# Grouped-query attention on one Trainium2 core: VectorE turns the keys of units 4, 7, 10 and every third up to 28, q1 starts in unit 3, query weights come by halves of the heads, and o is scaled in one instruction

## The chip, the cores and the metric

The kernel runs on one core of a Trainium2 chip. The metric is the device time of one execution in microseconds. Six runs of the kernel before took 185.41 to 186.72 us, with a median of 185.89 us. Engines are named as in the profile: PE (TensorE, with PEld for its weight loads), DVE (VectorE), ACT (ScalarE), POOL (GpSimd) and SP (SyncE, which issues nearly all loads).

## The reference

```python
B, Sq, D = 8, 32, 1024
Hq, Hkv, Sk, Dh = 32, 4, 8192, 128
W = 2048                                   # min(4096, max(256, Sk // 4))
q = (x @ wq) split into 32 heads of 128
k, v = the last W positions of k_cache, v_cache; each of the 4 kv heads serves 8 query heads
scores = q @ k^T * Dh ** -0.5
o = softmax(scores) @ v
out = o (heads side by side, 4096 wide) @ wo
```

All inputs and the output are bf16.

## The kernel before, in words

The work is 32 units: one unit is one batch row b and one kv head g, with the eight batch rows of g = 0 first. A unit has 256 query columns (8 heads x 32 positions) and 2048 keys, which are 16 blocks of 128. It runs in four *slots* (the loop over `c` in `run`, lines 462 to 488), so there are 128 slots. In a slot PE makes the transposed scores of four key blocks (L467, `s_ps`: K turned is the stationary side, q the moving side), ACT takes exp into `pT` (L469), and PE multiplies `pT` of two slots earlier with `va` (L478, `o_ps`). `va` is V with a column of ones beside it, so `o_ps` also holds the sum of the exponentials. `va_copy` (L409) copies V there on DVE at the start of each unit, into one of three buffers. When a unit's last product is issued, `finish_unit` (lines 411 to 424) runs on DVE: a reciprocal of the sums (L415), two scalings of 128x128 into `o_sb` (L420), and a transpose in blocks of 32 into `OT` (L422).

The other work of PE is cut into pieces that are put in slots behind the slot's own matmuls:

- `q_pieces` (lines 267 to 280) make q of the next kv head g: per head two pieces of four 128x256 matmuls (L275) and one DVE copy into `QT` (L278). `Q_SLOTS` (L30) spreads the 16 pieces of g = 1 over slots 17 to 31. A head of g needs both halves of that head group's weights, which are halves of the contraction (`load_wq`, L156), rows of 2 KB.
- `o_pieces` (L282) multiply finished heads with `wo` (L295) and add into `oacc`.
- `k_pieces` (lines 224 to 239) turn the keys of the units in `PE_T` on PE, four 128x128 transposes in each slot of the unit before (L236), and DVE copies half a unit at a time from PSUM to `kT` (L238).

Keys come in transposed in one of three ways. Units in `PE_T` are turned by PE from a plain load (`k_raw`). Units in `V_T` are turned by DVE and POOL from a plain load (`kv_pieces`, lines 241 to 262): four DVE transposes in blocks of 32 (L251), then sixteen moves of 32x512 that put the blocks in their places. A move reads a part of all four transposed pieces, so none can start before the fourth. In `V_T` stand, for each unit, the unit whose load brings `k_raw` along, the slots of the four transposes, the first and last slot of the moves, and how many of the moves POOL does (L261); DVE does the rest (L259). All other units use the DMA's transposing load, in two halves (L196).

Every engine's order is that in which the program is written: a slot's side pieces decide where an instruction stands in its engine's queue. SP issues the loads in the order of `load_unit` (line 207), about five units ahead; `W_AT` (L28) says with which unit each of 28 pieces of weights is issued. An SP instruction waits for a free buffer and for the transfer eight before it.

Buffers that matter: 2 for `k_raw` of units 0 and 1 and for `kTv` (the result of `kv_pieces`), 4 for other `k_raw`, 5 for `kT`, 6 for V, 6 for weights, 2 PSUM banks each for scores, `o_ps` pairs and side work.

Of the kernel before, what the change touches and what calls it, by code (L numbers as in the profile page):

```python
# [9 lines left out]
ALU = mybir.AluOpType  # L10
AX = mybir.AxisListType
BF16 = mybir.dt.bfloat16
FP32 = mybir.dt.float32
# [7 lines left out]
VA_ROW = 160  # L21
V_HALVES = 30

PE_T = (0, 1, 2, 3, 4)

V_T = {5: (2, (5, 6, 8, 10), 10, 17, 12),
       **{u: (u - 4, range(4 * u - 16, 4 * u - 12), 4 * u - 13, 4 * u - 4, 16) for u in (8, 11, 14, 17, 20, 23, 26, 29)}}
W_AT = (3, 3, 4, 4, 8, 8, 9, 9, 11, 12, 13, 13, 14, 15, 16, 16, 18, 19, 19, 20, 22, 22, 23, 24, 25, 26, 28, 28)  # L28

Q_SLOTS = {1: (17, 31), 2: (38, 54), 3: (69, 83)}  # L30
O_SLOTS = {0: (54, 71), 1: (84, 101), 2: (99, 123), 3: (124, 143)}


# [71 lines left out]
class Fast:  # L105
# [50 lines left out]
    def load_wq(self, g, half, cuts=(2, 2)):  # L156
# [8 lines left out]
                                   in_=self.wq[:, g * GW:(g + 1) * GW].rearrange("(p c) n -> p c n", p=P)[:, c0:c0 + n, :])  # L165
        return [lambda i=sum(cuts[:k]), n=n: piece(i, n) for k, n in enumerate(cuts)]

    def load_wo(self, gq):

        def piece(i):  # L170
            if i == 0:
                self.wo_t[gq] = self.wp.tile([self.P, 4, self.D], BF16, name="wo_sb", tag="w")
            r0 = gq * 4 * self.Dh
            self.nc.sync.dma_start(out=self.wo_t[gq][:, 2 * i:2 * i + 2, :],
                                   in_=self.wo[r0:r0 + 4 * self.Dh, :].rearrange("(p c) n -> p c n", c=4)[:, 2 * i:2 * i + 2, :])
        return [lambda i=i: piece(i) for i in range(2)]
# [30 lines left out]
    def load_unit(self, ui):  # L207

        if ui < len(self.units):
            if ui not in V_T:  # L210
                self.load_k(ui, None if ui in PE_T else 0)
            self.load_v(ui, self.nc.sync)
            if ui not in V_T and ui not in PE_T:
                self.load_k(ui, 1)
        for u, at in V_T.items():
            if at[0] == ui:
                self.load_k(u)
        for p, at in zip(self.weights, W_AT):
            if at == ui:
                p()  # L220

    def k_pieces(self, ui):

        if ui not in PE_T:
            return []
# [13 lines left out]
    def kv_pieces(self, ui):  # L241


        nc, P, KT = self.nc, self.P, self.KT
        st = {}

        def blocks(i):
            if i == 0:
                st["kb"] = self.kbp.tile([P, KT, P], BF16, name="kb")
            sl = slice(i * KT // 4, (i + 1) * KT // 4)  # L250
            nc.vector.transpose(out=st["kb"][:, sl, :], in_=self.k_raw[ui][:, sl, :])  # L251

        def move(k, d):
            if k == d == 0:
                self.kT[ui] = self.kvt.tile([P, KT, P], BF16, name="kTv", tag="kv")
            out = self.kT[ui][d * 32:(d + 1) * 32, :, k * 32:(k + 1) * 32]
            in_ = st["kb"][k * 32:(k + 1) * 32, :, d * 32:(d + 1) * 32]
            if d >= V_T[ui][4] // 4:
                nc.vector.tensor_copy(out=out, in_=in_)  # L259
            else:  # L260
                nc.gpsimd.tensor_scalar(out=out, in0=in_, scalar1=1.0, scalar2=1.0, op0=ALU.mult, op1=ALU.mult)  # L261
        return [lambda i=i: blocks(i) for i in range(4)], [lambda k=k, d=d: move(k, d) for k in range(4) for d in range(4)]
# [4 lines left out]
    def q_pieces(self, g):  # L267
        nc, P, DC = self.nc, self.P, self.DC
        st = {}

        def piece(hl, i):
            if i == 0:
                st["ps"] = self.ps_m.tile([P, 512], FP32, name="q_ps", tag="m")
            for c in range(i * DC // 2, (i + 1) * DC // 2):
                nc.tensor.matmul(st["ps"][:, 0:self.NQ], lhsT=self.wq_t[g, i][:, c % (DC // 2), hl * P:(hl + 1) * P],  # L275
                                 rhs=self.xT[:, c, :], start=(c == 0), stop=(c == DC - 1))
            if i == 1:
                nc.vector.tensor_copy(out=self.q_view(g)[:, :, hl, :],  # L278
                                      in_=st["ps"][:, 0:self.NQ].rearrange("p (b s) -> p b s", b=self.B))
        return [lambda h=h, i=i: piece(h, i) for h in range(self.rep) for i in range(2)]  # L280

    def o_pieces(self, g, t, cuts=(512, 512), st=None):  # L282
# [29 lines left out]
    def start(self):  # L312
        nc, P = self.nc, self.P
# [18 lines left out]
        self.weights = []  # L332
        for g in range(self.Hkv):
            if g + 1 < self.Hkv:
                self.weights += self.load_wq(g + 1, 0) + self.load_wq(g + 1, 1)
            if g:
                self.weights += self.load_wo(2 * g - 2) + self.load_wo(2 * g - 1)
        self.weights += self.load_wo(2 * self.Hkv - 2) + self.load_wo(2 * self.Hkv - 1)
        for ui in range(2, 4):
            self.load_unit(ui)  # L340
        for v in self.va:
            nc.gpsimd.memset(v[:, :, self.Dh:self.VW], 1.0)
        nc.gpsimd.memset(self.ones_c[:, :], 1.0)
# [67 lines left out]
    def finish_unit(self, ui, o_ps):  # L411
        nc, P, Dh, QT_N = self.nc, self.P, self.Dh, self.QT_N
        b, g = self.units[ui]
        rl = self.RL_all
        nc.vector.reciprocal(out=rl[:, ui * QT_N:(ui + 1) * QT_N], in_=o_ps[:, :, Dh])  # L415
        if ui == len(self.units) - 1:
            self.check_units(ui, ui + 1)
        o_sb = self.ob.tile([P, QT_N, 4, 32], BF16, name="o_sb")
        for qt in range(QT_N):
            nc.vector.tensor_scalar(out=o_sb[:, qt, :, :], in0=o_ps[:, qt, 0:Dh].rearrange("p (i c) -> p c i", c=4),  # L420
                                    scalar1=rl[:, ui * QT_N + qt:ui * QT_N + qt + 1], scalar2=None, op0=ALU.mult)
        nc.vector.transpose(out=self.OT[:, g * QT_N:(g + 1) * QT_N, :, b * self.Sq:(b + 1) * self.Sq], in_=o_sb[:, :, :, :])  # L422
        if ui == len(self.units) - 2:
            self.check_units(0, ui + 1)
# [20 lines left out]
    def run(self):  # L445
        nc, P, NCH, CJ, UQ, QT_N, KT = self.nc, self.P, self.NCH, self.CJ, self.UQ, self.QT_N, self.KT
        self.start()
        plan = self.side_plan()
        for i, p in enumerate(self.q_rest):
            plan[i // 2].append(p)  # L450
        pv_queue = []

        loads = {8: [4, 5, 6, 7], **{4 * (u - 5): [u] for u in range(8, len(self.units))}}

        for ui, (b, g) in enumerate(self.units):
            nxt = self.k_pieces(ui + 1)
            va = self.va[ui % 3]
            if ui:
                self.va_copy(ui)
            q_u = self.QT[g][:, b * UQ:(b + 1) * UQ]  # L460
            acc = {}
            for c in range(NCH):
                for u in loads.get(ui * NCH + c, []):
                    self.load_unit(u)
                s_ps = self.ps_s.tile([P, CJ, UQ], FP32, name="s_ps")
                for jj in range(CJ):
                    nc.tensor.matmul(s_ps[:, jj, :], lhsT=self.kT[ui][:, c * CJ + jj, :], rhs=q_u, start=True, stop=True)  # L467
                pT = self.ptp.tile([P, CJ, UQ], BF16, name="pT")
                nc.scalar.activation(out=pT[:, :, :], in_=s_ps[:, :, :], func=ACT.Exp, bias=0.0, scale=self.scale)  # L469

                def pv(c=c, pT=pT, acc=acc, va=va, ui=ui):
                    if c == 0:
                        acc["o"] = self.ps_o.tile([P, QT_N, 256], FP32, name="o_ps")
                    o_ps = acc["o"]
                    for jj in range(CJ):
                        j = c * CJ + jj
                        for qt in range(QT_N):
                            nc.tensor.matmul(o_ps[:, qt, 0:self.VW], lhsT=pT[:, jj, qt * P:(qt + 1) * P], rhs=va[:, j, 0:self.VW],  # L478
                                             start=(j == 0 and qt == 0), stop=(j == KT - 1), skip_group_check=True)
                    if c == NCH - 1:  # L480
                        self.finish_unit(ui, o_ps)
                pv_queue.append(pv)
                while len(pv_queue) > 2:
                    pv_queue.pop(0)()
                for k in ((c,) if ui else ((), (), (0, 1), (2, 3))[c]) if nxt else ():
                    nxt[k]()
                for p in plan[ui * NCH + c]:
                    p()
        after = [p for s in range(len(self.units) * NCH, len(plan)) for p in plan[s]]
        pv_queue.pop(0)()  # L490
        for p in after[:2]:
            p()
        self.pv_last, self.after = pv_queue.pop(0), after[2:]
# [162 lines left out]
```

## Time and profile before

| | |
|---|---|
| median of 6 runs | 185.89 us (185.41 to 186.72) |
| the profiled execution | 185.5 us |
| its span (first to last instruction) | 183.7 us |
| granted TensorE clock | 0.999 |
| L467 scores, PE | 368 + 144 matmuls of 128x256 |
| L478 products with V, PE | 1024 matmuls of 128x129 |
| L236 transposes of keys, PE | 64 of 128x128 |
| L469 exp, ACT | 128 x 1025 ns |
| L261 moves, POOL | 140, 669 ns mean |
| L420 scaling, DVE | 64 x 346 ns |
| L278 q copies, DVE | 24 x 407 ns |

A row of a timeline has the start and the length in microseconds, the engine, the line, the operation, what is written and read, how often, and in brackets the idle time before it with what ended it. A group row has the busy time, the mean of one in ns, and after the second bar the idle time. Matmuls overlap, so their lengths add to more than the time; the distance between two starts is what one costs. Slot 12 below is the thirteenth group of score matmuls from the start; slots 16 and 20 begin units 4 and 5.

### The profile page before, as it was taken

To read this page: it belongs to the slowest core of one execution; us is meant where nothing else is said; L and a number is where in the kernel's file an instruction comes from. 1 tells how busy PE (TensorE), PEld (TensorE's weight loads), DVE (VectorE), ACT (ScalarE), POOL (GpSimd) and SP (SyncE) were. 2 spreads that over 40 slices of the span, in tenths; PEclk is the share of its full clock that TensorE was granted. 3 is DMA by queue.
4 is the path that set the end of the run, shared out by engine and by line. 5 is a ranking of instruction groups with operands and counts; after the bars stand their busy time and mean duration, and the time that the engine had idled before them with its cause. 6 is when DMAs were issued, how large, how long until landed. Compare 5 with 4: busy or idle time off the path is not lost.

```text
span 183.7 us, 5041 instructions
## 1 busy us (share of the span) xinstructions
PE 179.4 (98%) x2041; PEld 154.0 (84%) x2057; DVE 115.8 (63%) x266; ACT 131.6 (72%) x133; POOL 94.6 (51%) x150
## 2 busy tenths in 40 slices
PE   8999999999999999999999999999999999999994
PEld 2999999999999999987878999988787888888843
DVE  0238899986685685685467558647755865365363
ACT  2208898777889787878787677787877888888800
POOL 2000009759839959929944980796299279600000
PEclk9999999999999999999999999999999999999999
DMA  5999999999999999999999999999999999990003
GB/s 193 331 411 407 400 401 379 199 210 385 268 338 253 345 298 206 393 266 318 302 380 252 338 375 236 283 261 414 231 326 400 251 270 337 241 234 9 0 30 91
DMA packets 52953, 51.72 MB, mean 282 GB/s; under 512 B 39744, under 2 KB 40256, under 8 KB 52928
## 3 DMA queue, kind: packets, MB, share of 16 engines
q1 hardware_dynamic: 52352, 50.90, 99.6%
q10 hardware_dynamic: 576, 0.49, 0.8%
q8 instruction: 15, 0.25, 0.5%
q14 instruction: 10, 0.08, 0.2%
HBM read 41.42 MB, written 0.52 MB: 228 GB/s over the span
## 4 chain that ended last, share of the span: by engine, by line
PE 98%; issue 0%; DVE 0%
PE o_ps L478 32%; PE s_ps L467 31%; PE op_ps L295 14%; PE q_ps L275 11%; PE q_ps L375 4%; PE tp L236 2%; PE warm_ps L346 2%; PE xT_ps L354 1%; PE kf_ps L368 1%; DVE o_t L305 0%; PE cnt_ps L532 0%
## 5 line engine op out<-in xcount | busy, mean ns | idle before, releaser
L469 ACT ACTIVATE pT<-s_ps 128x1024 bf16<-128x1024 f32 x128 | 128.7, 1025 | 32.7 <-PE s_ps L467 31.8
L261 POOL TENSOR_SCALAR kTv<-kb 32x512 bf16<-32x512 bf16 x140 | 93.7, 669 | 64.4 <-PE s_ps L467 37.6
L478 PE MATMUL o_ps<-va,pT 128*128 128x129 bf16 x1024 | 78.8, 220 | 0.1
L478 PEld LDWEIGHTS <-pT 128*128 128x128 bf16 x1024 | 68.5, 98 | 3.1
L467 PE MATMUL s_ps<-QT,kT 128*128 128x256 bf16 x368 | 55.2, 273 | 0.2
L467 PEld LDWEIGHTS <-kT 128*128 128x128 bf16 x368 | 34.8, 98 | 10.3
L295 PE MATMUL op_ps<-wo_sb,OT 128*128 128x512 bf16 (+2 forms) x128 | 32.7, 353 | 0.6
L275 PE MATMUL q_ps<-xT,wq_sb 128*128 128x256 bf16 x192 | 28.2, 273 | 0.0
L409 DVE COPY va<-v_sb 128x2048 bf16<-128x2048 bf16 x32 | 26.1, 817 | 0.1
L251 DVE STREAM_TRANSPOSE kb<-k_raw 128x512 bf16<-128x512 bf16 x36 | 23.8, 685 | 0.5 <-DMA k_raw<-in_k_cache_dram 0.4
L415 DVE RECIPROCAL RL_all<-o_ps 128x2 f32<-128x2 f32 x32 | 5.3, 164 | 27.0 <-PE o_ps L478 27.0
L467 PE MATMUL s_ps<-QT,kTv 128*128 128x256 bf16 x144 | 21.6, 273 | 0.0
L420 DVE TENSOR_SCALAR o_sb<-o_ps,RL_all 128x128 bf16<-128x128 f32 x64 | 19.5, 346 | 1.1
L467 PEld LDWEIGHTS <-kTv 128*128 128x128 bf16 x144 | 13.9, 98 | 5.1
L275 PEld LDWEIGHTS <-wq_sb 128*128 128x128 bf16 x192 | 17.0, 98 | 1.2
L278 DVE CAST QT<-q_ps 128x256 bf16<-128x256 f32 x24 | 9.8, 407 | 12.7 <-PE q_ps L275 12.7
L422 DVE STREAM_TRANSPOSE OT<-o_sb 128x256 bf16<-128x256 bf16 x32 | 14.2, 445 | 1.1
L295 PEld LDWEIGHTS <-OT 128*128 128x128 bf16 x144 | 11.4, 98 | 2.3 <-DVE OT L422 0.2
L302 DVE TENSOR_TENSOR oacc<-op_ps,oacc 128x512 f32<-128x512 f32 x8 | 5.5, 682 | 7.4 <-PE op_ps L295 7.4
L375 PE MATMUL q_ps<-xT,wq_sb 128*128 128x256 bf16 (+1 forms) x80 | 7.8, 251 | 0.0
L375 PEld LDWEIGHTS <-wq_sb 128*128 128x128 bf16 x80 | 6.6, 98 | 0.7 <-DMA wq_sb<-in_wq_dram 0.2
L236 PE MATMUL tp<-ident,k_raw 128*128 128x128 bf16 x64 | 5.9, 219 | 0.0
(30 smaller groups left out, 37.6 us busy)
## 6 DMA issues: line engine op xcount, KB each, us to landing
v_sb<-in_v_cache_dram SPq DMA_DIRECT2D x30, 512.0 KB, 7.2
wo_sb<-in_wo_dram SPq DMA_DIRECT2D x16, 512.0 KB, 6.9
wq_sb<-in_wq_dram SPq DMA_DIRECT2D x13, 512.0 KB, 7.2
k_raw<-in_k_cache_dram SPq DMA_DIRECT2D x13, 512.0 KB, 6.4
wq_sb<-in_wq_dram SPq DMA_DIRECT2D x6, 256.0 KB, 4.9
v_sb<-in_v_cache_dram SPq DMA_DIRECT2D x4, 256.0 KB, 4.2
kT<-in_k_cache_dram SPq DMA_TRANSPOSE x36, 7.1
k_raw<-in_k_cache_dram SPq DMA_DIRECT2D x2, 256.0 KB, 6.7
```

What stands on the lines that cost most here:

```text
L251: nc.vector.transpose(out=st["kb"][:, sl, :], in_=self.k_raw[ui][:, sl, :])
L261: nc.gpsimd.tensor_scalar(out=out, in0=in_, scalar1=1.0, scalar2=1.0, op0=ALU.mult, op1=ALU.mult)
L275: nc.tensor.matmul(st["ps"][:, 0:self.NQ], lhsT=self.wq_t[g, i][:, c % (DC // 2), hl * P:(hl + 1) * P], rhs=self.xT[:, c, :], start=(c == ...
L278: nc.vector.tensor_copy(out=self.q_view(g)[:, :, hl, :], in_=st["ps"][:, 0:self.NQ].rearrange("p (b s) -> p b s", b=self.B))
L295: nc.tensor.matmul(ps[:, 0:w], lhsT=self.OT[:, gq, c, t * P:(t + 1) * P], rhs=self.wo_t[gq][:, c, n0:n0 + w], start=(k == 0), stop=(k == 7))
L375: nc.tensor.matmul(qs[h // 2][:, h % 2, n0:n1], lhsT=self.wq_t[0, c // H][:, c % H, h * P:(h + 1) * P], rhs=self.xT[:, c, n0:n1], start=(c ...
L409: self.nc.vector.tensor_copy(out=self.va[ui % 3][:, :, 0:self.Dh], in_=self.v_sb[ui][:, :, :])
L420: nc.vector.tensor_scalar(out=o_sb[:, qt, :, :], in0=o_ps[:, qt, 0:Dh].rearrange("p (i c) -> p c i", c=4), scalar1=rl[:, ui * QT_N + qt:ui ...
L422: nc.vector.transpose(out=self.OT[:, g * QT_N:(g + 1) * QT_N, :, b * self.Sq:(b + 1) * self.Sq], in_=o_sb[:, :, :, :])
L467: nc.tensor.matmul(s_ps[:, jj, :], lhsT=self.kT[ui][:, c * CJ + jj, :], rhs=q_u, start=True, stop=True)
L469: nc.scalar.activation(out=pT[:, :, :], in_=s_ps[:, :, :], func=ACT.Exp, bias=0.0, scale=self.scale)
L478: nc.tensor.matmul(o_ps[:, qt, 0:self.VW], lhsT=pT[:, jj, qt * P:(qt + 1) * P], rhs=va[:, j, 0:self.VW], start=(j == 0 and qt == 0), stop= ...
```

## The change: which engine turns which keys, and what moves with it

`PE_T` loses unit 4: it is now turned by DVE and POOL, with six of its sixteen moves on DVE. The other units of `V_T` are 7, 10, ... 28 instead of 8, 11, ... 29, with four of the sixteen moves on DVE instead of none, spread evenly among POOL's. Unit 5 had twelve moves on POOL; it now comes by a transposing load, and so do 8, 11, ... 29. So 19 units come by transposing loads (18 before) and four units are turned on PE (five before).

The pieces of q1 start in slot 14. Query weights of g = 1 to 3 are loaded by halves of the heads, in rows of 1 KB, and q of two heads is copied at once, by ACT. The second half of q1's weights is issued with unit 5 instead of unit 4, and weights now go ahead of `k_raw` of the same load. `k_raw` of unit 4 is loaded directly behind that of unit 2. From unit 12 on `va_copy` stands one slot earlier. The two scalings of a unit become one `tensor_tensor` with the reciprocals broadcast.

```diff
-PE_T = (0, 1, 2, 3, 4)
-V_T = {5: (2, (5, 6, 8, 10), 10, 17, 12),
-       **{u: (u - 4, range(4 * u - 16, 4 * u - 12), 4 * u - 13, 4 * u - 4, 16) for u in (8, 11, 14, 17, 20, 23, 26, 29)}}
-W_AT = (3, 3, 4, 4, 8, 8, 9, 9, 11, ...
-Q_SLOTS = {1: (17, 31), 2: (38, 54), 3: (69, 83)}
+PE_T = (0, 1, 2, 3)
+V_T = {4: (None, (6, 6, 7, 8), 8, 15, 10),
+       7: (4, (15, 16, 17, 18), 18, 26, 12),
+       **{u: (u - 4, range(4 * u - 15, 4 * u - 11), 4 * u - 12, 4 * u - 3, 12) for u in range(10, 31, 3)}}
+W_AT = (3, 3, 5, 5, 8, 8, 9, 9, 11, ...
+V_EARLY = 12
+Q_SLOTS = {1: (14, 31), 2: (38, 54), 3: (69, 83)}
...
+    def load_wq_heads(self, g, half):
+        P, DC, GW = self.P, self.DC, self.rep * self.Dh
+        n0 = g * GW + half * GW // 2
+        def piece(i):
+            if i == 0:
+                self.wq_t[g, half] = self.wp.tile([P, DC, GW // 2], BF16, name="wq_sb", tag="w")
+            cs = slice(i * DC // 2, (i + 1) * DC // 2)
+            self.nc.sync.dma_start(out=self.wq_t[g, half][:, cs, :],
+                                   in_=self.wq[:, n0:n0 + GW // 2].rearrange("(p c) n -> p c n", p=P)[:, cs, :])
+        return [lambda i=i: piece(i) for i in range(2)]
...
-            if d >= V_T[ui][4] // 4:
+            i, n = 4 * k + d, 16 - V_T[ui][4]
+            if i * n // 16 != (i + 1) * n // 16:
                 nc.vector.tensor_copy(out=out, in_=in_)
...
-            if i == 0:
-                st["ps"] = self.ps_m.tile([P, 512], FP32, name="q_ps", tag="m")
+            k, R = hl // 2, self.rep // 2
+            if i == 0 and hl % 2 == 0:
+                st["ps"] = self.ps_m.tile([P, 2, self.NQ], FP32, name="q_ps", tag="m")
...
-            if i == 1:
-                nc.vector.tensor_copy(out=self.q_view(g)[:, :, hl, :],
-                                      in_=st["ps"][:, 0:self.NQ].rearrange("p (b s) -> p b s", b=self.B))
+            if i == 1 and hl % 2 == 1:
+                nc.scalar.copy(out=self.q_view(g)[:, :, 2 * k:2 * k + 2, :].rearrange("p b h s -> p h b s"),
+                               in_=st["ps"][:, :, :].rearrange("p h (b s) -> p h b s", b=self.B))
...
-        for ui in range(2, 4):
-            self.load_unit(ui)
+        self.load_k(2)
+        self.load_k(4)
+        self.load_v(2, nc.sync)
+        self.load_unit(3)
...
-        for qt in range(QT_N):
-            nc.vector.tensor_scalar(out=o_sb[:, qt, :, :], in0=o_ps[:, qt, 0:Dh].rearrange("p (i c) -> p c i", c=4),
-                                    scalar1=rl[:, ui * QT_N + qt:ui * QT_N + qt + 1], scalar2=None, op0=ALU.mult)
+        nc.vector.tensor_tensor(out=o_sb[:, :, :, :], in0=o_ps[:, :, 0:Dh].rearrange("p q (i c) -> p q c i", c=4),
+                                in1=rl[:, ui * QT_N:(ui + 1) * QT_N].unsqueeze(2).unsqueeze(3).to_broadcast([P, QT_N, 4, 32]), op=ALU.mult)
...
-            if ui:
+            if 0 < ui < V_EARLY:
                 self.va_copy(ui)
...
+                if c == NCH - 1 and V_EARLY <= ui + 1 < len(self.units):
+                    self.va_copy(ui + 1)
```

More of the change, by code (lines that the diff above doesn't have):

```diff
@@ L22 @@
 V_HALVES = 30
-PE_T = (0, 1, 2, 3, 4)
-V_T = {5: (2, (5, 6, 8, 10), 10, 17, 12),
-       **{u: (u - 4, range(4 * u - 16, 4 * u - 12), 4 * u - 13, 4 * u - 4, 16) for u in (8, 11, 14, 17, 20, 23, 26, 29)}}
-W_AT = (3, 3, 4, 4, 8, 8, 9, 9, 11, 12, 13, 13, 14, 15, 16, 16, 18, 19, 19, 20, 22, 22, 23, 24, 25, 26, 28, 28)
-Q_SLOTS = {1: (17, 31), 2: (38, 54), 3: (69, 83)}
+PE_T = (0, 1, 2, 3)
+V_T = {4: (None, (6, 6, 7, 8), 8, 15, 10),
+       7: (4, (15, 16, 17, 18), 18, 26, 12),
+       **{u: (u - 4, range(4 * u - 15, 4 * u - 11), 4 * u - 12, 4 * u - 3, 12) for u in range(10, 31, 3)}}
+W_AT = (3, 3, 5, 5, 8, 8, 9, 9, 11, 12, 13, 13, 14, 15, 16, 16, 18, 19, 19, 20, 22, 22, 23, 24, 25, 26, 28, 28)
+V_EARLY = 12
+Q_SLOTS = {1: (14, 31), 2: (38, 54), 3: (69, 83)}
 O_SLOTS = {0: (54, 71), 1: (84, 101), 2: (99, 123), 3: (124, 143)}
@@ L214, in load_unit @@
                 self.load_k(ui, 1)
+        for p, at in zip(self.weights, W_AT):
+            if at == ui:
+                p()
         for u, at in V_T.items():
@@ L217, in load_unit @@
                 self.load_k(u)
-        for p, at in zip(self.weights, W_AT):
-            if at == ui:
-                p()
     def k_pieces(self, ui):
@@ L271, in piece @@
         def piece(hl, i):
-            if i == 0:
-                st["ps"] = self.ps_m.tile([P, 512], FP32, name="q_ps", tag="m")
+            k, R = hl // 2, self.rep // 2
+            if i == 0 and hl % 2 == 0:
+                st["ps"] = self.ps_m.tile([P, 2, self.NQ], FP32, name="q_ps", tag="m")
             for c in range(i * DC // 2, (i + 1) * DC // 2):
-                nc.tensor.matmul(st["ps"][:, 0:self.NQ], lhsT=self.wq_t[g, i][:, c % (DC // 2), hl * P:(hl + 1) * P],
-                                 rhs=self.xT[:, c, :], start=(c == 0), stop=(c == DC - 1))
-            if i == 1:
-                nc.vector.tensor_copy(out=self.q_view(g)[:, :, hl, :],
-                                      in_=st["ps"][:, 0:self.NQ].rearrange("p (b s) -> p b s", b=self.B))
+                nc.tensor.matmul(st["ps"][:, hl % 2, :], lhsT=self.wq_t[g, hl // R][:, c, (hl % R) * P:(hl % R + 1) * P],
+                                 rhs=self.xT[:, c, :], start=(c == 0 and hl % 2 == 0), stop=(c == DC - 1), skip_group_check=True)
+            if i == 1 and hl % 2 == 1:
+                nc.scalar.copy(out=self.q_view(g)[:, :, 2 * k:2 * k + 2, :].rearrange("p b h s -> p h b s"),
+                               in_=st["ps"][:, :, :].rearrange("p h (b s) -> p h b s", b=self.B))
         return [lambda h=h, i=i: piece(h, i) for h in range(self.rep) for i in range(2)]
@@ L334, in start @@
             if g + 1 < self.Hkv:
-                self.weights += self.load_wq(g + 1, 0) + self.load_wq(g + 1, 1)
+                self.weights += self.load_wq_heads(g + 1, 0) + self.load_wq_heads(g + 1, 1)
             if g:
```

## The prediction, made before the changed kernel was run

> **What bounds the kernel now.** I read the page first: busy shares, DMA rows, chain by engine.
>
> ```profile
> PE 179.4 (98%) x2041; PEld 154.0 (84%) x2057; DVE 115.8 (63%) x266; ACT 131.6 (72%) x133; POOL 94.6 (51%) x150
> DMA  5999999999999999999999999999999999990003
> GB/s 193 331 411 407 400 401 379 199 210 385 268 338 253 345 298 206 393 266 318 302 380 252 338 375 236 283 261 414 231 326 400 251 270 337 241 234 9 0 30 91
> PE 98%; issue 0%; DVE 0%
> ```
>
> TensorE is the chain. But the DMA engines are full as well, from 5 us to about 167 us: two resources run side by side, and the second holds only a few us in reserve.
>
> Next, TensorE's timeline around unit 3, where unit 4's K is turned (slots 12 to 15), and at slot 16, which has no side work.
>
> ```profile
> 26.41 0.39 PE L236 MATMUL tp<-ident,k_raw 128*128 128x128 bf16 x4
> 26.63 0.60 PE L467 MATMUL s_ps<-QT,kT 128*128 128x256 bf16 x4
> 27.07 0.62 PE L478 MATMUL o_ps<-va,pT 128*128 128x129 bf16 x8
> 27.68 0.40 PE L236 MATMUL tp<-ident,k_raw 128*128 128x128 bf16 x4
> 27.91 0.60 PE L467 MATMUL s_ps<-QT,kT 128*128 128x256 bf16 x4
> ...
> 31.25 0.60 PE L467 MATMUL s_ps<-QT,kT 128*128 128x256 bf16 x4
> 31.69 0.62 PE L478 MATMUL o_ps<-va,pT 128*128 128x129 bf16 x8
> 32.15 0.60 PE L467 MATMUL s_ps<-QT,kT 128*128 128x256 bf16 x4
> ```
>
> A slot with four transposes is 1.115 us (slots 5 to 11), one without side work 0.89-0.90 (31.25 to 32.15), one with a q piece 1.33. Slot 12 took 1.28: its transposes waited for k_raw of unit 4, which landed at 27.64.
>
> Last, VectorE and GpSimd before the first VectorE unit, then two group rows.
>
> ```profile
> 19.93 0.17 DVE L415 RECIPROCAL RL_all<-o_ps 128x2 f32<-128x2 f32 x1 [0.76 <-PE o_ps L478]
> 20.13 0.61 DVE L420 TENSOR_SCALAR o_sb<-o_ps,RL_all 128x128 bf16<-128x128 f32 x2
> ...
> 22.93 0.65 DVE L238 COPY kT<-tp 128x1024 bf16<-128x1024 bf16 x1
> 23.50 0.68 DVE L409 COPY va<-v_sb 128x2048 bf16<-128x2048 bf16 x1
> 24.10 0.70 DVE L251 STREAM_TRANSPOSE kb<-k_raw 128x512 bf16<-128x512 bf16 x1
> ...
> 26.48 0.69 DVE L251 STREAM_TRANSPOSE kb<-k_raw 128x512 bf16<-128x512 bf16 x1
> ```
>
> ```profile
> 27.33 8.77 POOL L261 TENSOR_SCALAR kTv<-kb 32x512 bf16<-32x512 bf16 x12 [25.76 <-PE s_ps L467]
> 38.73 11.69 POOL L261 TENSOR_SCALAR kTv<-kb 32x512 bf16<-32x512 bf16 x16 [2.63 <-PE s_ps L467]
> ```
>
> ```profile
> L305 DVE TENSOR_TENSOR o_t<-op_ps,oacc 128x256 bf16<-128x256 f32 x1 | 0.4, 425 | 0.1
> L259 DVE COPY kTv<-kb 32x512 bf16<-32x512 bf16 x4 | 1.8, 449 | 0.1
> ```
>
> From 19.93 on VectorE has no gap until slot 12 is over. GpSimd starts 0.85 us after the last block transpose starts (26.48 to 27.33), and every move reads all four blocks. Its twelve moves end at 36.10; unit 5's first score matmul is at 36.56, so that turn had 0.46 us to spare.
>
> **The change, part by part.** *Unit 4 leaves TensorE.* Four slots lose 1.115 - 0.89 = 0.225 each: -0.90. The wait in slot 12 goes with them: 1.28 - 1.115 = -0.17. Together -1.07. What is late next is kTv of unit 4.
>
> *When TensorE wants it.* Slot 12 at 26.63; slots 12 and 13 bare (0.89 each), 14 and 15 with a q1 piece (1.33 each): slot 16 at 31.07.
>
> *When it is there.* VectorE's order after the reciprocal at 19.93, by the steps between starts in the timeline: reciprocal 0.20, joint scaling 0.47, OT transpose 0.36, kT copy 0.58, two blocks 1.21, kT copy 0.57, block 0.62, va copy 0.60. The last block thus starts at 24.54, and GpSimd 0.85 later, at 25.39. Ten moves at 8.77/12 = 0.73 are 7.3: done at 32.7. VectorE's six moves (0.45 to 0.6 each) stand between finish_unit(1), two kT copies, va(3) and finish_unit(2); adding the same steps, the last ends near 32.3. k_raw of unit 4 is no cause: second in its queue, it lands near 19.8, and the blocks start at 21.5. So slot 16 begins near 32.6, a new wait of +1.5. Part may show earlier: kT(3)'s first copy moves from 25.90 to about 26.6, ends 27.25 and delays slot 12 by 0.6; that is inside the same 1.5, as GpSimd's end does not move. Bounds: 0.9 (short GpSimd moves of 0.67 only, VectorE 0.3 early) and 2.0 (VectorE moves at 0.6).
>
> *A rule against the moves.* The Trainium skill, GPSIMD Engine Reference, section "Key points", says that GpSimd shares its SBUF interfaces with VectorE and contends with VectorE's two-port modes. The rows say who pays: VectorE's moves took 288 to 609 ns, va copies 651 alone and up to 1136 beside GpSimd, while GpSimd's moves have a median of 612 ns whatever VectorE does. If GpSimd were held for the six moves, kTv would come 6 x 0.3 = 1.8 us later; by the row it is not. I take the row.
>
> *Units 7, 10, ... 28.* Twelve GpSimd moves are 8.8 us instead of 11.7, within the 13 to 16 us between their last block and their unit (unit 10: blocks near 49, done near 58, wanted at 60.6). VectorE gains 38 - 4 = 34 moves x 0.45 = +15.3, loses 24 q copies x 0.41 = -9.8, two kT copies -1.3, and 32 x (0.61 - 0.43) = -5.8: about -1.6 net. Cost nothing: VectorE keeps about a third of its time free, and TensorE needs its results slots later.
>
> *Joint scaling.* The trace lacks this form. Below: one 128x128 scaling, 346 ns; above: the 128x512 tensor_tensor, 682. I take 425, the 256-wide row. Only the last unit's stands near the end, where TensorE waits 0.2 for OT: -0.1.
>
> *q copies on ScalarE.* Twelve of 128x512; near row: ScalarE's xT copy of 128x512, 586 ns; above, an exp of twice the width, 1025. Take 0.6. Behind each waits the next exp. Exps follow each other every 0.905 at best; four slots with q are 5.3 and need 3.6 + 0.6. Hidden, cost 0; at 1.0 still hidden.
>
> *va copy a slot earlier, from unit 12.* It can now wait for v (v of 15 lands at 84.75; slot 59 is at 85.78). Behind it on VectorE stand moves, op_ps adds and finish_unit; TensorE wants their results slots later. Cost 0.
>
> *DMA.* On SP's queue unit 5's K (1.28 us of DMA, the step between landings) becomes two transposing halves, typically 0.88 each: +0.5 once; unit 4's load is only earlier, v of unit 2 one transfer later (21.1, wanted 24). The second half of wq1 goes behind unit 5's K: it lands near 35, wanted at slot 22, about 40. Query weights now come in rows of 1 KB. The Trainium skill, DMA: Bandwidth & Descriptors, "Specifications", asks only for 512 B or more for line rate: no cost. The trace's 1024-byte packets (only output stores) took 48 ns, its 2048-byte ones 84: 14% more, 0.17 per piece. Ahead of unit 15's K stand nine such pieces at most: by the page +0.5 in all, by the row 0.5 + 9 x 0.17 = +2.0. The tightest landing before is unit 15's second K half, at 87.04 (issue 85.3 plus 6.0), wanted at slot 62, at 89.74: 2.7 of reserve. I take the row: about 1 left, since TensorE is itself later by then. Cost 0.
>
> **Sum.** -1.07 + 1.5 - 0.1 = +0.3. The profiled execution took 185.5 us (span 183.7 and 1.8 around it): 185.8. The median of the runs shown is 185.89, 0.4 above that execution, so 186.2.
>
> **Rivals.** (1) *Likeliest, 0.60:* the wait at slot 16 gives back the transposes; 186.2, own range 185.4 to 187.0. (2) *kTv is in time, 0.20:* if VectorE reaches the last block and its own moves 1.5 us sooner, all of -1.17 stays: 184.7. For: VectorE's steps come from one execution, and before, twelve moves met their slot with 0.46 us over. Against: it had no gap to lose. (3) *DMA late, 0.20, on the slower side:* the place is units 14 to 17, score matmuls waiting for a transposed K half. It decides once the DMA added ahead of unit 15 passes 2.7 plus TensorE's own 0.4: with 0.5 for unit 5, about 0.29 per wq piece (row: 0.17). At 0.4 per piece, 0.5 + 3.6 = 4.1 stands against 3.1, the half is 1.0 us late, and the time is 187.2. For: single landing steps of 2.3 to 2.9 us occur, so the reserve can be thinner than one number tells.
>
> **Numbers.** A measurement of this kernel tells about 0.5% (0.93 us) from no change: faster is below 184.96, slower above 186.82. Case 1 gives 0.50 same, 0.09 slower, 0.01 faster; case 2 0.17 faster, 0.03 same; case 3 0.20 slower. So faster 0.18, same 0.53, slower 0.29. Range 184.7 to 187.5.
>
> **What would show it.** L236 with 48 instead of 64 matmuls; ten POOL moves from about 25.4 to 32.7, and the first score matmuls on unit 4's kTv near 32.6 with TensorE idle before them; slot 31 near 52.1 (before 51.59); ScalarE copies near 0.6 that nobody waits for; no DMA named ahead of PE or PEld after 35 us. Wrong if slot 16 starts by 31.3, or if s_ps waits for kT's DMA.

## The result: 0.7% slower, and the profile after

| | before | after |
|---|---|---|
| median of the runs | 185.95 us (38 runs, 185.19 to 187.69) | 187.37 us (17 runs, 186.61 to 188.68) |
| ratio, 95% interval | | 1.0072 (1.0052 to 1.0091) |
| median of the runs' spans | 183.8 to 183.9 us (four chips, 80 runs beside the experiments) | 185.1 us (19 runs) |
| profiled execution, span | 185.5, 183.7 us | 186.74, 185.0 us |

The two profiled spans differ by 1.24 us, the medians of the spans by 1.2 to 1.3 and the medians of the times by 1.42, so the pair of traces can be read for nearly the whole difference. Ratios, here and below, leave out executions more than 1.5% above the fastest of their kernel. Lines of `kernel.py` are now 15 to 20 higher: L487 scores, L498 products, L251 transposes, L253 kT copies, L428 va copy, L275 and L277 the moves on VectorE and GpSimd.

First the page after: the engines, and the share of the chain of waits by engine.

```profile
PE 178.7 (97%) x2025; PEld 152.6 (83%) x2041; DVE 117.4 (63%) x242; ACT 135.9 (73%) x145; POOL 71.0 (38%) x116
...
PE 81%; DMA 8%; DVE 7%; issue 1%; SPq 1%
```

TensorE did 0.7 us less work and ended 1.24 us later. The chain of before was 98% PE; now VectorE has 7% of it and the DMA 8%. The chain itself, in order of time (start, length, what), shows where:

```profile
9.29 9.35 DMA k_raw<-in_k_cache_dram
...
20.22 0.44 DVE o_sb L438
...
32.07 0.63 DVE kTv L275
32.84 0.60 PE s_ps L487 x4
```

The DMA share is the start, up to 18.6, where before waited for the same load (slot 5 is only 0.09 later). VectorE's share is one piece: from 20.22 to 32.84 the links are VectorE, and from there on TensorE. TensorE's timeline says what that cost (from the transposes of slot 11 to slot 16; matmuls overlap, so read the starts).

```profile
26.50 0.39 PE L251 MATMUL tp<-ident,k_raw 128*128 128x128 bf16 x4
27.38 0.61 PE L487 MATMUL s_ps<-QT,kT 128*128 128x256 bf16 x4 [0.50 <-DVE kT L253]
27.83 0.62 PE L498 MATMUL o_ps<-va,pT 128*128 128x129 bf16 x8
...
29.17 0.60 PE L487 MATMUL s_ps<-QT,kT 128*128 128x256 bf16 x4
30.06 0.61 PE L498 MATMUL o_ps<-va,pT 128*128 128x129 bf16 x8 [0.29 <-DVE va L428]
...
31.84 0.60 PE L292 MATMUL q_ps<-xT,wq_sb 128*128 128x256 bf16 x4
32.84 0.60 PE L487 MATMUL s_ps<-QT,kTv 128*128 128x256 bf16 x4 [0.40 <-DVE kTv L275]
```

Three waits stand here. Slot 12 starts 0.88 after its predecessor's transposes, where 0.22 was usual: 0.67 lost to the first kT copy of unit 3. The products of slot 14 start 0.89 after its scores (29.17 to 30.06), where 0.45 is usual (27.38 to 27.83): 0.45 for va of unit 3. Slot 16 starts 1.00 after its q piece, where 0.44 is usual: 0.56 for kTv of unit 4. The sum is 1.68. The brackets show less (0.50, 0.29, 0.40), since the matmuls before are modelled as ending late; a distance between starts is the safer figure.

VectorE in the same stretch is one queue, without a gap from 20.02 to 34.6:

```profile
20.02 0.17 DVE L434 RECIPROCAL RL_all<-o_ps 128x2 f32<-128x2 f32 x1 [1.11 <-PE o_ps L498]
...
24.02 0.65 DVE L428 COPY va<-v_sb 128x2048 bf16<-128x2048 bf16 x1
24.59 0.70 DVE L266 STREAM_TRANSPOSE kb<-k_raw 128x512 bf16<-128x512 bf16 x1
...
26.68 0.65 DVE L253 COPY kT<-tp 128x1024 bf16<-128x1024 bf16 x1
...
28.97 1.04 DVE L428 COPY va<-v_sb 128x2048 bf16<-128x2048 bf16 x1
...
31.77 0.92 DVE L275 COPY kTv<-kb 32x512 bf16<-32x512 bf16 x2
```

```profile
25.46 7.08 POOL L277 TENSOR_SCALAR kTv<-kb 32x512 bf16<-32x512 bf16 x10 [23.89 <-DVE kb L266]
```

Each of the three late results is in that queue or starts from it: the kT copy at 26.68, the va copy at 28.97, the last two moves at 31.77 (done 32.69), and GpSimd's ten, which begin 0.87 after the last block transpose starts and end at 32.54.

A comparison of slot starts in the two traces completes the account: slot 5 is +0.09, slot 31 is +0.70, slot 33 is +0.80, and slots 34 to 127 are all +0.81. From there nothing is lost or won until the last matmul. But the span is 1.24 longer, so 0.44 more is lost behind the last matmul. The spans end with eight short waits on SP, one for each of the semaphores over which the DMAs go in turn, 0.06 us apart where nothing holds them:

```
                         before    after
last output store lands  182.82   183.62
first of the 8 checks    181.29   183.64
last of the 8 checks     182.84   184.08
span ends                183.72   184.96
landing to end             0.89     1.34
```

Before, the last store belonged to the semaphore that is looked at last; seven checks were done before it landed. After, it belongs to the first one, and seven checks of 0.063 us (0.44 in all) come behind it. The page's issue rows say why:

```profile
k_raw<-in_k_cache_dram SPq DMA_DIRECT2D x12, 512.0 KB, 7.1
...
kT<-in_k_cache_dram SPq DMA_TRANSPOSE x38, 6.8
```

These were 13 and 36 before: one DMA more in all, so every later one moves on by one of eight semaphores.

### The profile page after: what moved, and what is told of

Same layout as the page of the kernel before. It is cut to its first block, busy times and chain, and to the rows that moved or that the text cites. A ratio compares the mean times of both kernels' runs of the same rounds, so it can differ in the third digit from the quotient of the medians.

```text
span 185.0 us, 4971 instructions
## 1 busy us (share of the span) xinstructions
PE 178.7 (97%) x2025; PEld 152.6 (83%) x2041; DVE 117.4 (63%) x242; ACT 135.9 (73%) x145; POOL 71.0 (38%) x116
## 4 chain that ended last, share of the span: by engine, by line
PE 81%; DMA 8%; DVE 7%; issue 1%; SPq 1%
PE o_ps L498 28%; PE s_ps L487 28%; PE op_ps L312 14%; PE q_ps L292 11%; DMA k_raw<-in_k_cache_dram 5%; DMA wq_sb<-in_wq_dram 3%; DVE kTv L275 1%; DVE kT L253 1%; DVE kb L266 1%; SPq L166 1%; DVE va L428 1%; DVE OT L440 1%; DVE o_sb L438 1%; DVE RL_all L434 0%; PE tp L251 0%
## 5 line engine op out<-in xcount | busy, mean ns | idle before, releaser
L277 POOL TENSOR_SCALAR kTv<-kb 32x512 bf16<-32x512 bf16 x106 | 70.0, 661 | 81.1 <-DVE kb L266 65.2
L498 PE MATMUL o_ps<-va,pT 128*128 128x129 bf16 x1024 | 78.8, 220 | 0.3 <-DVE va L428 0.3
L498 PEld LDWEIGHTS <-pT 128*128 128x128 bf16 x1024 | 68.5, 98 | 3.5 <-issue 0.5
L487 PE MATMUL s_ps<-QT,kT 128*128 128x256 bf16 x368 | 55.2, 272 | 0.8 <-DVE kT L253 0.5
L487 PEld LDWEIGHTS <-kT 128*128 128x128 bf16 x368 | 34.9, 98 | 11.5 <-DVE kT L253 0.7
L312 PE MATMUL op_ps<-wo_sb,OT 128*128 128x512 bf16 (+2 forms) x128 | 32.7, 353 | 0.4
L428 DVE COPY va<-v_sb 128x2048 bf16<-128x2048 bf16 x32 | 26.1, 817 | 2.3 <-DMA v_sb<-in_v_cache_dram 1.8
L487 PE MATMUL s_ps<-QT,kTv 128*128 128x256 bf16 x144 | 21.6, 273 | 0.5 <-DVE kTv L275 0.4
L487 PEld LDWEIGHTS <-kTv 128*128 128x128 bf16 x144 | 13.9, 98 | 5.4 <-POOL kTv L277 0.6
L275 DVE COPY kTv<-kb 32x512 bf16<-32x512 bf16 x38 | 17.3, 454 | 0.8
L438 DVE TENSOR_TENSOR o_sb<-o_ps,RL_all 128x256 bf16<-128x256 f32 x32 | 13.6, 424 | 1.1
L295 ACT CAST QT<-q_ps 128x512 bf16<-128x512 f32 x12 | 7.0, 581 | 0.0
```

Of the source, the lines that this page charges most:

```text
L312: nc.tensor.matmul(ps[:, 0:w], lhsT=self.OT[:, gq, c, t * P:(t + 1) * P], rhs=self.wo_t[gq][:, c, n0:n0 + w], start=(k == 0), stop=(k == 7))
L428: self.nc.vector.tensor_copy(out=self.va[ui % 3][:, :, 0:self.Dh], in_=self.v_sb[ui][:, :, :])
L438: nc.vector.tensor_tensor(out=o_sb[:, :, :, :], in0=o_ps[:, :, 0:Dh].rearrange("p q (i c) -> p q c i", c=4), in1=rl[:, ui * QT_N:(ui + 1) ...
```

## Experiments

**Theory A:** 0.81 us (less some jitter of the start) comes from VectorE's queue between 20 and 33 us, and 0.44 from the DMA count. **Rivals:** the end differs by chance from execution to execution; a moved part (q1's place, the scaling, ScalarE's q copies) costs the time by itself; the DMA engines, full in both kernels, are what limits, and the waits on VectorE only stand in front. All times of slots below are against the profiled execution of before; ratios are against runs of before on the same chip.

**1 and 2. One DMA less in after, one more in before.** `V_HALVES` decides how many of the last units load V in two halves.

```diff
-V_HALVES = 30
+V_HALVES = 31     # e1_one_load_less, in the kernel after; e2_before_one_load_more: 29, in the kernel before
```

> The changed kernel with V of unit 30 loaded in one transfer instead of two, so that the program has one DMA fewer and the last output store falls on the last of the eight DMA semaphores again, as before. Theory A (of the 1.3 us, 0.81 is waiting at slots 12 to 16 net of the transposes and 0.44 is the order in which SP checks the eight semaphores at the end): slot 127 stays within 0.2 us of 173.5, the time from the last store's landing to the end of the span falls from 1.3 to about 0.9 us, ratio to before about 1.0045 to 1.005. Theory B (all of it is the waiting, the end is chance): no change, ratio 1.007.

> The kernel before with V of unit 29 loaded in two halves: one DMA more, nothing else. Theory A: the last store moves to the semaphore that SP checks first, seven more checks of about 0.06 us stand behind it, +0.44 us, ratio 1.002 to 1.0025. Theory B: ratio 1.000.

| | landing to end | slot 127, against its base | median span | ratio to before |
|---|---|---|---|---|
| after | 1.34 | | 185.1 | 1.0072 |
| e1_one_load_less | 0.89 | -0.04 | 184.55 | 1.0053 (1.0034 to 1.0073) |
| before | 0.89 | | 183.9 | 1 |
| e2_before_one_load_more | 1.34 | +0.03 | 184.25 | 1.0017 (0.9994 to 1.004) |

The end moved by 0.44 both ways and the slots did not move. The medians of the spans agree (0.55 less than after, 0.35 more than before); the ratio of the second by itself would not exclude 1. That the DMA count sets 0.44 us of the end is shown.

**3. Unit 4 back on TensorE**, all else as after.

```diff
-PE_T = (0, 1, 2, 3)
-V_T = {4: (None, (6, 6, 7, 8), 8, 15, 10),
-       7: (4, ...
+PE_T = (0, 1, 2, 3, 4)
+V_T = {7: (4, ...
...
-        self.load_k(4)
```

> The changed kernel with unit 4 turned by TensorE again, as before (k_raw of unit 4 loaded with its unit), all else as changed. Theory A (unit 4's turn on VectorE and GpSimd makes the waits at slots 12, 14 and 16, 1.68 us in all; each of four slots gets its transposes back, +0.9): slot 31 about 0.8 us earlier than in the changed kernel, 51.5, ratio about 1.003. Rival (DMA lateness or ScalarE's q copies or VectorE's new moves in the later units cost the time): the loss stays, ratio 1.007 or more.

Measured: ratio 1.0095 (1.006 to 1.0131) of six runs, two of which have spans of 186.3 and 186.9 us, the others 184.7 to 185.2. In the profiled one (184.7) the waits at slots 12, 14 and 16 are gone, as expected, but slot 31 is at +0.49, not near 0 (in kernels without the early load of unit 4, lines are one or two lower):

```profile
29.81 0.39 PE L250 MATMUL tp<-ident,k_raw 128*128 128x128 bf16 x4
30.63 0.60 PE L291 MATMUL q_ps<-xT,wq_sb 128*128 128x256 bf16 x4 [0.44 <-DVE kT L252]
```

The first q1 piece waits 0.6 for a PSUM bank: q pieces and turned K share two of them, both hold K of unit 4, and the copy that frees one is in VectorE's queue. The expectation missed this. So q1 from slot 14 and unit 4 on TensorE can't be had together without a wait; this run alone doesn't give the price of unit 4.

**4. q1 from slot 10**, to see whether filling TensorE earlier hides the waits.

```diff
-Q_SLOTS = {1: (14, 31), ...
+Q_SLOTS = {1: (10, 26), ...
```

> The changed kernel with the 16 pieces of q1 in slots 10 to 25, one in each: six of them stand before slot 16 instead of two, 1.74 us of work that has to be done anyway. Theory A: the waits at slots 12 to 16 fall from 1.68 to at most 0.3 us, slot 31 is near 50.9, and the ratio near 1.000, if the DMA reserve of 1.24 us at unit 15 does not run out first; if it does (the score matmuls wait for a transposed K half at units 14 to 17), up to 0.5 us is given back there. Rival (kTv of unit 4 is late by more than work can fill): slot 16 goes later by the four pieces' 1.74 us and nothing is gained.

Measured: 1.0074 (1.0046 to 1.0102), slot 31 at +0.90 where about -0.7 was expected. All three waits vanish and one takes their place:

```profile
25.34 0.39 PE L251 MATMUL tp<-ident,k_raw 128*128 128x128 bf16 x4
27.33 0.60 PE L292 MATMUL q_ps<-xT,wq_sb 128*128 128x256 bf16 x4 [1.61 <-DVE kT L253]
```

Again the bank, again the kT copy of unit 3. The slot comes 1.77 late (1.99 between the starts shown, 0.22 usual), in one piece against 1.68 in three: this order of TensorE's work changed where it waits, and hardly how long.

**5. q1 from slot 12**, with one DMA less as in experiment 1: late enough for the bank, early enough to be work while kTv is made.

```diff
-V_HALVES = 30
+V_HALVES = 31
-Q_SLOTS = {1: (14, 31), ...
+Q_SLOTS = {1: (12, 28), ...
```

> The changed kernel with the pieces of q1 in slots 12 to 27, one in each, and one load less (V of unit 30 whole). At slot 12 the PSUM bank that a q piece takes is freed by the same kT copy that slot 12 waits for anyway, so two more pieces (0.87 us) can stand in front of slot 16 without the block that slot 10 met. Theory A: the wait at slot 12 stays (0.67), those at slots 14 and 16 fall from 1.0 to about 0.2, slot 31 near 51.5, end of span 0.44 sooner, ratio about 1.000 to 1.001. Rival (VectorE's queue holds TensorE up wherever q stands): slot 31 stays near 52.3, ratio 1.005.

Measured: 1.0017 (0.9984 to 1.005), level with before. The wait at slot 12 stays 0.67, that at slot 16 shrinks to 0.15, slot 31 is at -0.13. But four of twelve spans are 185.5 to 186.5 us, the others 183.6 to 184.4. (*Late*, from here on, is an execution whose span is more than 1.5 us above the shortest of its kernel.) The profiled one is the longest, so its waits show a place, not a typical size:

```profile
PEld L487 <- DMA kT<-in_k_cache_dram: 3.2, 6, 1.5
```

(Waits: total us, times, longest.) TensorE now loses 2.0 us waiting for transposed halves of K, at slots 80 to 86 (116 to 125 us), and 0.7 us at slot 79 for a va copy that waits for V. That is rival 3 of the prediction, at units 20 and 21 instead of 14 to 17.

In the profiled execution of after it stays away: the smallest reserve, from the landing of a transposed half to its first score matmul, is 1.0 us there (unit 17), and TensorE is 0.83 us later than here (slot 31: +0.70 against -0.13). But one execution tells a reserve badly: experiment 1, the same program as after up to unit 30, has 2.1 us, and experiment 2, that of before up to unit 29, has 3.2 where before has 2.7. And just ahead of the waits one transfer of `wo` takes 4.04 us from landing to landing (at 109.0 us), where before, after and experiment 9 have no step over 3.1 between 12 and 168 us. What makes such a step stays open.

**6. Unit 4 by the transposing DMA**, q1 from 14. It takes the six moves, the four block transposes and GpSimd's ten away, and adds 0.5 us of DMA (two halves of 0.89 between landings for one load of 1.29). With `V_HALVES` at 31 the number of DMAs is that of after.

```diff
-V_T = {4: (None, (6, 6, 7, 8), 8, 15, 10),
-       7: (4, ...
+V_T = {7: (4, ...
...
-        self.load_k(4)
```

> The changed kernel with unit 4 loaded by the transposing DMA, turned by no engine, and one load less. Theory A: the waits at slots 12 to 16 are gone and the transposes too, slot 31 is near 50.6 (1.0 before that of the kernel before); but the DMA engines get another 0.5 us of work, unit 15's second K half lands near 89.8, and TensorE would want it at 88.8: so about 1 us comes back as waits of score matmuls for K at units 14 to 17, and the end is within 0.3 us of the kernel before, ratio 0.999 to 1.001. Rival (the DMA reserve is larger than the landings say): the whole microsecond stays, ratio 0.995.

Measured: 1.0055 (1.002 to 1.0089). Up to slot 31 it is as expected, -1.00: without the work of turning unit 4, VectorE's queue delays nobody. Then the DMA is late (the profiled span is 186.2 us; the shortest of twelve was 183.9):

```profile
89.13 0.61 PE L485 MATMUL s_ps<-QT,kT 128*128 128x256 bf16 x4 [1.28 <-DMA kT<-in_k_cache_dram]
```

That is slot 60, unit 15, the tightest transfer that the prediction had named. Slot 127 is at +2.0. Of the 2.9 us lost between slots 33 and 60 this wait is half; 1.2 is at slot 43, for a va copy that stands behind a block transpose whose k_raw has not landed, and 0.2 at slot 38, for another half of K. Nor does the -1.00 reach the end in the shortest execution: 183.8 - 1.0 + 0.44 would be 183.2. So VectorE's queue is what after waits for, and close behind it, 1 us away in these traces, stands the DMA.

**7. Unit 4 on TensorE and q1 from 17 as before**, one DMA less: only the parts that no one has accused stay (units 7 to 28, joint scaling, ScalarE's q copies, 1 KB rows, va a slot earlier).

> The changed kernel with unit 4 on TensorE and q1 from slot 17 as before, and one load less. What stays of the change: the later units' turns with VectorE moves, query weights by heads, q copies on ScalarE, early va copies, joint scaling. Theory A: the whole loss is unit 4's turn, q1's place and the order of the end; every slot is within 0.1 us of the kernel before, ratio 1.000. Rival (one of the staying parts costs time): slots fall behind after slot 31, ratio 1.003 or more.

Measured: 1.0043 (1.0007 to 1.0079). In the profiled execution (span 184.2, late by 0.6 at slot 0 already) TensorE waits for nobody after 20 us, and slot 5 to slot 127 takes 0.09 less than in before. But VectorE's wait for V shows what has thinned:

```profile
DVE va L426 <- DMA v_sb<-in_v_cache_dram: 13.2, 12, 2.2
```

Twelve waits, where before has none and after three of 1.8 us in all. Seven of the twelve spans are 183.5 to 184.4; the other five, 185.5 to 187.1. Those five have no trace; that they wait for the DMA is inferred from experiment 5.

**8. Two scalings again**, one run.

```diff
-        nc.vector.tensor_tensor(out=o_sb[:, :, :, :], ...
+        for qt in range(QT_N):
+            nc.vector.tensor_scalar(out=o_sb[:, qt, :, :], ...
```

> The changed kernel with two scalings of 128x128 per unit instead of the joint one. Theory A (VectorE's queue has no gap from 20 to 33 us, each scaling in it shifts unit 4's moves): two finish_units stand before the last block transpose's successors, one of them before the block itself, so slots 12 to 16 wait 0.2 to 0.4 us more, slot 31 near 52.6; later slots do not lose more, since VectorE is a third idle there. Rival (the joint form is worth 0.18 us per unit everywhere): the loss grows with the units.

Measured (188.45 us): the waits at slots 12 and 14 grow to 1.04 and 0.93, that at slot 16 is 0.43 (by distances of starts, 2.40 in all, 0.72 more than in after, where 0.2 to 0.4 was expected). From slot 5 to slot 31 this kernel loses 1.35 us against before, after 0.61. The joint scaling is worth 0.74 us, all of it between 20 and 33 us, where VectorE is the bound; elsewhere nothing.

**9. Query weights of g = 2 and 3 in rows of 2 KB again**, on top of experiment 5. If the 1 KB rows thin the reserve, the late executions must go.

```diff
...
-                self.weights += self.load_wq_heads(g + 1, 0) + self.load_wq_heads(g + 1, 1)
+                load = self.load_wq_heads if g == 0 else self.load_wq
+                self.weights += load(g + 1, 0) + load(g + 1, 1)
```

> The kernel with q1 from slot 12 and one load less, and the query weights of g = 2 and 3 loaded again as halves of the contraction, in rows of 2 KB (those of g = 1 stay by heads). Theory A (the rows of 1 KB cost about 0.2 us of DMA each, and that is what makes some executions wait for K at units 15 to 27): the five pieces ahead of unit 15 land about 1 us sooner in all, the smallest reserve grows from 0 to about 1 us, the executions above 185 us of span vanish or become rare, median span 183.8, ratio 1.000. Rival (the extra transposing loads thin the reserve, the rows do not): four of twelve executions stay above 185.

Measured: 0.9995 (0.9971 to 1.002), all twelve spans 183.5 to 184.2, none late, where experiments 5 and 7 had nine late ones in 24. The smallest reserve is 1.4 us. VectorE waits for V once, for 0.2 us. Experiments 5 and 7 ran on another chip, though. Before had no late execution there (29 runs) and one here (17), so the chip alone doesn't bring them, but the comparison on one chip is missing. Nor do the 1 KB rows always bring them: after had two in 19, experiment 3 two in six, experiments 1 and 4 none in 18. That the rows make executions late is likely by this, and not shown.

**10. Unit 4 by DMA with all query weights in 2 KB rows, q1 from 17.** If only the rows kept experiment 6 from its gain, this should have it.

> Unit 4 by the transposing DMA, one load less, all query weights in rows of 2 KB with the second half of q1's issued with unit 4 and q1 from slot 17, as in the kernel before. Theory A: no waits at slots 12 to 16 and no transposes of unit 4, so slots from 31 on stand 1.0 us before those of the kernel before where the DMA allows it; two more units than before come transposed (+1.0 us of DMA), so of the 2.7 us of reserve 0.7 is left: span near 182.8, ratio 0.995, with a few executions near 184. Rival (two more transposing units take more than 0.5 us each): K is late at units 14 to 17 and the ratio is 1.000 or above.

Measured: 1.0097 (1.006 to 1.0134): the expectation failed. (Two of six spans, 188.0 and 189.3 us at granted clocks of 0.99 and 0.98, are not in the ratio; the number of DMAs is that of after, so 0.44 of the end is.) Slot 16 is at -1.18, and then:

```profile
34.56 0.61 PE L496 MATMUL o_ps<-va,pT 128*128 128x129 bf16 x8 [1.20 <-DVE va L426]
```

```profile
33.22 0.71 DVE L265 STREAM_TRANSPOSE kb<-k_raw 128x512 bf16<-128x512 bf16 x1 [3.65 <-DMA k_raw<-in_k_cache_dram]
33.85 0.65 DVE L426 COPY va<-v_sb 128x2048 bf16<-128x2048 bf16 x1
```

The va copy of unit 4 had its V, but stands behind a block transpose of unit 7, whose k_raw lands at 33.2 only. The wait at the head of VectorE's queue became TensorE's wait 1.3 us later. A wait for q1's weights at 61.1 and one for va at 64.9 follow. What unit 4 by DMA would give with k_raw of unit 7 in time was not tried.

**11. q copies on VectorE instead of ScalarE**, one run.

```diff
-                nc.scalar.copy(out=self.q_view(g)...
+                nc.vector.tensor_copy(out=self.q_view(g)...
```

> The changed kernel with the twelve q copies of 128x512 on VectorE instead of ScalarE. Theory A: the first comes in slot 17, after unit 4's moves, so the waits at slots 12 to 16 stay within 0.1 us and slot 31 is at 52.3; later VectorE has gaps: no other slot changes by more than 0.1. Rival (ScalarE's copies delay exps and with them TensorE): slots 17 to 31 become faster by more than 0.1 us.

Measured (186.99 us): the three waits are the same to 0.01, and the later slots too, but for 0.09 at slots 31 to 33 that after loses and this kernel doesn't. Which engine copies q is worth at most 0.1.

**12. The va copy of unit 2 on GpSimd**, on top of experiment 9. It takes 0.57 us, the va copy at 24.02, out of VectorE's queue ahead of the last block transpose; GpSimd is idle then.

```diff
...
+        if ui == 2:
+            self.nc.gpsimd.tensor_scalar(out=out, in0=in_, scalar1=1.0, scalar2=1.0, op0=ALU.mult, op1=ALU.mult)
+        else:
+            self.nc.vector.tensor_copy(out=out, in_=in_)
```

> The kernel of the last call with q1 from slot 12, wide rows for g = 2 and 3 and one load less, and the va copy of unit 2 on GpSimd, which has nothing to do before 25.5 us (four times the elements per partition of a move: about 2.4 us, from 21.3 to 23.7; wanted at 24.9). Theory A (VectorE's queue from 20 to 33 us is what TensorE waits for): everything behind that copy on VectorE comes 0.57 us sooner, the wait at slot 12 falls from 0.67 to about 0.1 and that at slot 16 goes, slot 31 near 51.0 (with slot 5 at 18.9), median span near 183.1, ratio 0.995 to 0.997, some executions later where the DMA reserve of then 0.7 us is used up. Rival (GpSimd's copy takes so long, or slows VectorE so much, that unit 2's own product waits): a wait at slot 10, nothing gained, ratio 1.000 or more.

Measured: **184.97 us median (184.73 to 185.74, six runs), ratio 0.993 (0.9909 to 0.995)**, spans 182.8 to 183.2: faster than both kernels. By the spans the gain is smaller, 0.4% (median 183.05 against 183.8): the runs of before on this chip spend 2.5 us outside their spans, these 1.9, those on the other chips 1.8. VectorE, GpSimd and TensorE:

```profile
26.11 0.65 DVE L253 COPY kT<-tp 128x1024 bf16<-128x1024 bf16 x1
```

```profile
21.32 1.90 POOL L431 TENSOR_SCALAR va<-v_sb 128x2048 bf16<-128x2048 bf16 x1 [19.75 <-DMA v_sb<-in_v_cache_dram]
24.87 7.10 POOL L277 TENSOR_SCALAR kTv<-kb 32x512 bf16<-32x512 bf16 x10 [1.66 <-DVE kb L266]
```

```profile
26.53 0.39 PE L251 MATMUL tp<-ident,k_raw 128*128 128x128 bf16 x4
26.82 0.61 PE L492 MATMUL s_ps<-QT,kT 128*128 128x256 bf16 x4
```

The kT copy comes 0.57 earlier than in after (26.68 to 26.11), GpSimd's moves 0.59 earlier, the wait at slot 12 is 0.07 instead of 0.67, and slots 5 to 31 take 0.60 less than in experiment 9. The wait at slot 16, which was expected to go, stays at 0.14, since TensorE and kTv come earlier by the same amount. One instruction out of the queue moved the time by its whole length: the bound between 20 and 33 us is VectorE's queue.

## Why the prediction was right and wrong

The range held the time; the forecast itself was 1.2 us too low, and the likeliest class, no change, was not what came: the interval lies above 0.5%. The time is also above the range of its own case (185.4 to 187.0). What held it was the upper end that stands for a late DMA, and of that the profiled execution shows nothing: the range held in part by luck. Point by point:

- **What TensorE gains: -1.07, right.** Four slots of transposes and the wait in slot 12 for k_raw of unit 4 are gone. They are worth it when nothing else changes (experiment 6: -1.00 at slot 31).
- **The wait that takes their place: right in mechanism, 0.2 too small.** Slot 16 was put at 32.6 and came at 32.84; the last block transpose at 24.54 (24.59), GpSimd's moves from 25.4 to 32.7 (25.46 to 32.54), the kT copy at 26.6 (26.68). The term was 1.5; it measured 1.68, of which the kT copy's 0.67 was named as a part, and the 0.45 for va of unit 3 was not. It was summed as one wait at slot 16, though a late kT copy or va delays TensorE even where kTv would be in time: in experiment 5 the first stays at 0.67 while the last shrinks to 0.15.
- **GpSimd against VectorE: the price per move was right, the reading was not.** The Trainium skill, GPSIMD Engine Reference, "Key points", names contention on shared SBUF interfaces. It is there: the va copy took 0.65 us before GpSimd's moves began and 1.04 beside them. But VectorE doesn't pay alone, as the prediction read from the median of GpSimd's moves. Nine of the ten took 0.61 to 0.66 us and the one that began during the va copy 0.95; in before, a move began during each of 25 va copies and took 0.87 to 1.05 us, where none with VectorE idle took over 0.62. The 0.73 per move in the sum held two such moves in twelve, so it fitted (0.71 here).
- **Joint scaling: duration right (424 ns, forecast 425), worth misplaced.** At the tail, where -0.1 was put, it gave nothing: from the start of slot 127 to the landing of the last store it is 10.1 us in both. Its worth is 0.74 us in VectorE's full stretch (experiment 8), which the schedule of starts had in it without pricing it.
- **ScalarE's q copies: 581 ns (forecast 600); at most 0.1 instead of 0** (experiment 11). Units 7 to 28 and the earlier va copy: in the profiled execution TensorE never waits for them after slot 16.

```profile
L438 DVE TENSOR_TENSOR o_sb<-o_ps,RL_all 128x256 bf16<-128x256 f32 x32 | 13.6, 424 | 1.1
```

- **DMA: the row right in size, the reserve uncertain.** The step between landings of a query weight piece rose from 1.33 (median) to 1.54, +0.21 (forecast +0.17). The eight other kernels with all pieces in 1 KB rows have 1.50 to 1.55, the two with all in 2 KB rows 1.33 and 1.35. The Trainium skill, DMA: Bandwidth & Descriptors, "Specifications", has line rate from 512 B on, by which these rows would cost nothing; the measurement decides for the row. The smallest reserve fell from 2.7 to 1.0 (forecast about 1), but in single executions, and those of experiments 1 and 2 (2.1 and 3.2) show how far these differ. "DMA late" is not what made after slower, but by the traces of experiments 5 and 6 it is why taking the waits away brought no gain over before.
- **The term that was missing: +0.44 at the end.** The part on DMA counted transfers and their time, not what the number of DMAs does to the order of the last checks. With it the sum closes: -1.07 + 1.68 + 0.10 (slots 31 to 33) + 0.09 (slot 5 starts that much later) + 0.44 = 1.24, the difference of the spans. Without it the spans would differ by 0.8, and the ratio would have been near 1.004 or 1.005; experiment 1, without it, has 1.0053, its spans 0.65 above those of before.

The 0.09 at slot 5 is the landing of k_raw of unit 2, at 18.64 instead of 18.56; in the traces of the experiments slot 5 is anywhere from -0.15 to +0.58, so it is not told from chance. What stays open: what the late executions of after and of experiments 3 and 7 waited for, and whether the 1 KB rows make them.

## What to carry to other kernels

Before work is moved from the bound engine to another, make the list of that engine's queue in the very stretch where the result is due; a mean load of 63% says nothing about 13 us without a gap, and there an instruction taken away gave its whole length back. Ask next what is behind the wait (here a DMA reserve of 1 to 2 us, for which one trace is not enough), since a removed wait only pays up to there. And count what the change does to numbers that go in turn, the DMAs over their semaphores.

## What had not been expected of the hardware

- One DMA more or less in the program moved the end by 0.44 us: seven checks of 0.063 us ahead of, or behind, the last store's.
- Loads of 512 KB in rows of 1 KB took 16% more than in rows of 2 KB (1.54 against 1.33 us from landing to landing). Kernels with little DMA reserve had nine late executions in 24 with all query weights in such rows, and none in 12, on another chip, with a third of them.
- A move of GpSimd that began during VectorE's va copy took 0.87 to 1.16 us instead of 0.61, and such a copy up to 1.14 instead of 0.65: both engines lose time.
- GpSimd copied 128x2048 bf16 in 1.90 us, where VectorE needs 0.65 to 1.04; in a stretch where it idles that still paid.
